# A planned kernel whose plan is replaced by a table: attention with a window and sinks, then a two-layer MLP, on one core

## The chip, the core and the metric

The kernel runs on one core of one Trainium2 chip. The metric is the device time of one execution in microseconds. Three runs of the kernel before gave 209.28 (the median), 208.73 and 210.27 us. The engines are named as in the profile: PE is TensorE (matmuls; PEld are its weight loads), DVE is VectorE, ACT is ScalarE, POOL is GpSimd and SP is SyncE. A name with a q behind it (SPq, POOLq, DVEq) is the instruction queue of that engine, which also issues DMAs.

## The reference

Four batches, eight heads, 768 positions, head width 64. Each position attends to the 128 positions of its window and to four sinks at the start of its sequence. The result, 4 x 768 rows of 512, is normalised and goes through a two-layer MLP with a residual.

```python
scores = scale * np.matmul(q, k.transpose(0, 1, 3, 2))          # q, k, v: (4, 8, 768, 64), scale 1/8
keep = (pos[None, :] < 4) | ((rel >= 0) & (rel < 128))          # rel = row - column
a = softmax(np.where(keep, scores, -1e9))
x = np.matmul(a, v)                                             # heads side by side: (4, 768, 512)
xn = (x - mean) / np.sqrt(var + 1e-06) * g_ln
out = x + np.maximum(xn @ w_ch1, 0.0) @ w_ch2                   # 512 -> 2048 -> 512
```

## The kernel before

**Tiling.** The 3072 rows are 24 tiles of 128 (t = 0 to 23), two to a chunk (c = 0 to 11), three chunks to a batch. A chunk goes through: load of q, k and v (POOL issues these DMAs, which also turn float32 into bfloat16); transposition of q and k to the tile `kq` (on PE with an eviction for chunks 0 to 3, L595, L672; by transposing DMAs on SP, L569, after that); scores on PE into a double PSUM bank (`pair`, L754 for the first four tiles, L802 later); exponent on ACT (`pe`, L758 and L814); mask on DVE (L761, L826; one in four on POOL in the second half); values on PE (L854) with the sinks (L721); then on DVE the reciprocal (L868), the scaling to `x` (L870), the statistics (L874, L876) and, with a power on POOL (L882, L883), the normalised tile `xc` (L885). `xc` is transposed to `xnt` (on PE with an eviction at L893 and L907 for chunks 0 and 1, by a transposing DMA after that). The MLP's first layer (on PE, L1020 and L1027) is followed by a ReLU on ACT or DVE (L1037, L1039). Its second layer is a plain product for chunks 0 and 1 (L1058). From chunk 2 on the second layer, and from chunk 4 on half of the first, is done with seven products of half-size blocks in place of eight, with the sums of blocks made on DVE (L1092 `hs`, L1123 `tm`, L1130 `ot`, L980 `hq`), POOL (L938 `xt`) and ACT (L969 `tz`, L983, L1001). SP stores the result (L1070, L1154, L1159).

**Buffers.** Every kind of tile has a ring of buffers: two double PSUM banks `pair`, four single ones `one`, ten `pe`, four `ot` and so on. What may start depends on the inputs and on the buffer being free.

**What sets the order.** Every piece of work is declared as an operation with its possible engines, an estimated duration, a priority and the buffers that it reads and writes (`P.op`). `Plan.run` then plays the whole kernel through on these estimates: it takes the operation that can start first, chooses its engine and its buffer, and goes on. The result is a start for each operation, and the instructions are emitted sorted by it. On the chip each engine works through its own list in that order, and waits by semaphores for what it needs. Names used below: `av` values product of a tile, `ev` eviction of a transposed q/k tile, `evx` the same of a normalised tile, `ex` exponent, `mk` mask, `vs` the sink values of a batch (L707 for batch 0, L539 for the rest), `vcd` the 16 small loads of sink values (L535), `w2t` and `wsum` and `w1g` preparations of the weights on DVE or ACT (L1178, L923, L1190), `p1` to `p7` the seven products of the second layer (L1109).

**Fillers.** Where the plan leaves PE idle in the first 24 us, matmuls on a tile of zeros (`junk`, L1236) are put in, as many as fit into the planned gap.

**The end.** The last chunk's four half tiles are stored by SP one by one (L1154), a one-column matmul (`late`, L1206) stands last on PE, and a count of bad reciprocals made earlier decides by a branch (L1240) whether a general version of the kernel has to run, which it does not here.

## Time and profile before

| | us |
|---|---|
| three runs: median, lowest, highest | 209.28, 208.73, 210.27 |
| profiled execution: span from the first to the last instruction | 206.6 |
| PE busy in it | 199.4 (97%) |
| DVE, ACT, POOL busy in it | 179.6, 119.7, 118.7 |
| granted TensorE clock | 1.000 |

The page gives the profiled execution by its span; the median of the runs is 2.7 us above that span. Busy shares are averages over the whole span. The kernel has a head of some 19 us, in which PE waits or works on fillers, a long body, and a tail from the last product to the last store.

### The profile page before, as it was taken

Reading aid. Unit: us, or ns where it says so; the run is one execution under the profiler, and the core shown is the slowest. Engines: PE = TensorE matmul, PEld = TensorE weight load, DVE = VectorE, ACT = ScalarE, POOL = GpSimd, SP = SyncE. Lnnn points to the kernel's source line nnn. Section 1 sums busy time; section 2 is a strip of 40 time slices with the busy share of each in tenths; the row PEclk is TensorE's granted clock in tenths of the full one; section 3 lists DMA queues with packets and bytes.
Section 4 is the critical chain, followed back from the end, with each engine's and each line's share of the span. In section 5 each row is a group of like instructions: output and inputs, shape, how many; then the busy total and the mean of one; then the engine's idle time right before and its main releaser. Section 6 shows DMA issues by size and latency. Waiting matters only on the chain.

```text
span 206.6 us, 6790 instructions
## 1 busy us (share of the span) xinstructions
PE 199.4 (97%) x2766; PEld 165.6 (80%) x2766; DVE 179.6 (87%) x437; ACT 119.7 (58%) x187; POOL 118.7 (57%) x170
## 2 busy tenths in 40 slices
PE   6888999999999999999999999999999999999994
PEld 2557996674698897898998988988988988988993
DVE  7589769899599899899989989989989989998693
ACT  3649477839555655666486486485486585560620
POOL 7977475279039029959649949968627229125000
PEclk9999999999999999999999999999999999999999
DMA  5999999999999999999999999899976411210302
GB/s 117 146 195 195 197 181 205 199 158 171 186 200 124 124 191 101 121 174 101 175 152 137 113 159 143 109 171 114 194 117 101 128 33 23 106 32 19 108 27 84
DMA packets 101341, 27.55 MB, mean 133 GB/s; under 512 B 89652, under 2 KB 99128, under 8 KB 101304
## 3 DMA queue, kind: packets, MB, share of 16 engines
q0 software_dynamic: 67712, 13.37, 81.7%
q1 hardware_dynamic: 33304, 13.43, 34.1%
q8 instruction: 22, 0.36, 0.7%
q10 hardware_dynamic: 288, 0.26, 0.4%
q14 instruction: 15, 0.12, 0.2%
HBM read 27.31 MB, written 6.29 MB: 163 GB/s over the span
## 4 chain that ended last, share of the span: by engine, by line
PE 90%; DMA 3%; DVE 3%; POOL 2%; issue 0%; DVEq 0%
PE one L1109 31%; PE one L1027 20%; PE one L958 12%; PE one L1058 7%; PE one L1020 7%; PE pair L854 5%; PE pair L802 4%; DMA n4b<-in_q_dram 3%; PE one L672 1%; PE pair L721 1%; POOL nat L626 1%; PE one L714 1%; DVE xnt L907 1%; DVE kq L595 1%; POOL vn L589 0%; DVE st L874 0%
## 5 line engine op out<-in xcount | busy, mean ns | idle before, releaser
L1027 PE MATMUL one<-xnt,w 128*128 128x256 bf16 x384 | 46.8, 273 | 0.0
L814 ACT ACTIVATE pe<-pair 128x1024 bf16<-128x1024 f32 (+1 forms) x40 | 36.3, 963 | 18.2 <-PE pair L802 18.2
L1037 ACT ACTIVATE hq<-one 128x512 bf16<-128x512 f32 x58 | 33.4, 590 | 17.9 <-PE one L1020 9.4
L1027 PEld LDWEIGHTS <-w 128*128 128x128 bf16 x384 | 36.3, 98 | 4.0
L1109 PEld LDWEIGHTS <-hs 128*128 128x128 bf16 x320 | 31.0, 98 | 4.0
L882 POOL TENSOR_SCALAR st<-st 128x1 f32<-128x1 f32 x24 | 6.4, 266 | 44.4 <-DVE rec L868 27.5
L826 DVE TENSOR_TENSOR pe<-pe,mask 128x1024 bf16<-128x1024 bf16 (+1 forms) x35 | 27.1, 799 | 1.6 <-ACT pe L814 1.4
L969 ACT COPY tz<-one 128x512 f32<-128x512 f32 x24 | 13.9, 585 | 20.6 <-PE one L958 19.2
L1109 PEld LDWEIGHTS <-hq 128*128 128x128 bf16 x240 | 22.2, 98 | 4.1 <-issue 0.5
L589 POOL DMA_DIRECT2D vn<-in_v_dram x24 | 21.9, 922 | 2.2 <-DMA w<-in_moe_w_ch_dram 1.2
L983 ACT ACTIVATE hq<-hq 128x512 bf16<-128x512 bf16 x24 | 15.1, 630 | 13.1 <-DVE hq L980 12.6
L1109 PE MATMUL one<-w,hq 128*128 128x256 bf16 x160 | 19.2, 273 | 0.0
L980 DVE TENSOR_TENSOR hq<-one,tz 128x512 bf16<-128x512 f32 x24 | 16.4, 684 | 1.9 <-PE one L958 1.0
L1130 DVE TENSOR_TENSOR ot<-one,tm 128x256 f32<-128x256 f32 x40 | 15.9, 412 | 2.1 <-PE one L1109 1.8
L1123 DVE TENSOR_TENSOR tm<-one,x 128x256 f32<-128x256 f32 x40 | 16.6, 414 | 1.2 <-PE one L1109 1.1
L870 DVE TENSOR_TENSOR x<-pair,rec 128x512 bf16<-128x512 f32 x24 | 16.6, 691 | 0.8
L874 DVE BATCH_NORM_STATS2 st<-x 128x6 f32<-128x512 bf16 x24 | 16.5, 687 | 0.2
L1020 PE MATMUL one<-xnt,w 128*128 128x128 bf16 x256 | 16.0, 219 | 0.5 <-DVE xnt L907 0.5
L687 POOL DMA_DIRECT2D nat<-in_q_dram x16 | 14.2, 893 | 3.7 <-DMA w<-in_moe_w_ch_dram 3.7
L938 POOL TENSOR_TENSOR xt<-xnt 128x256 bf16<-128x256 bf16 x16 | 12.2, 778 | 7.1 <-DMA xnt<-xc 7.0
L687 POOL DMA_DIRECT2D nat<-in_k_dram x16 | 14.8, 928 | 2.4 <-DMA w<-in_moe_w_ch_dram 2.4
L1020 PEld LDWEIGHTS <-w 128*128 128x128 bf16 x256 | 14.6, 98 | 1.6 <-issue 0.8
(130 smaller groups left out, 387.7 us busy)
## 6 DMA issues: line engine op xcount, KB each, us to landing
out_dram<-ot SPq DMA_DIRECT2D x17, 256.0 KB
w<-in_moe_w_ch_dram POOLq DMA_DIRECT2D x8, 512.0 KB, 12.8
vn<-in_v_dram POOLq DMA_DIRECT2D x24, 128.0 KB, 6.9
nat<-in_k_dram POOLq DMA_DIRECT2D x17, 128.0 KB, 4.6
nat<-in_q_dram POOLq DMA_DIRECT2D x17, 128.0 KB, 4.9
out_dram<-ot SPq DMA_DIRECT2D x14, 128.0 KB
kq<-nat SPq DMA_TRANSPOSE x32
xnt<-xc SPq DMA_TRANSPOSE x20
```

Source lines behind the costliest of these rows:

```text
L589: loads[b * RB + r, "v"] = P.op(f"vld{t}", {"POOL": (0.87, 0.9)}, prio, lambda e: G.dma_start(bv.t[:, :, 0:64], v[b, :, 128 * r:128 * (r + ...
L687: lambda e, nat=nat, ap=ap: G.dma_start(nat.t, ap), writes=[nat], dma=SW if c < 6 else (*SW[:2], PAR["llag"]), after=behind(c, 0 if soon e ...
L814: P.op(f"ex{c}{hp}", {"ACT": act(2 * n)}, d + 0.1 + 0.05 * j, lambda e, pp=pp, pb=pb: nc.scalar.activation(pb.t[:, :, 0:n], pp.t[:, :, 0:n ...
L826: V.tensor_mul(pb.t[:, :, 0:n], pb.t[:, :, 0:n], mm),
L870: P.op(f"x{t}", {"DVE": dve(512)}, d + xo + 0.11, lambda e: V.tensor_tensor(x.t.rearrange("p (a h c) -> p a h c", a=2, c=64), pv()[:, :, : ...
L874: P.op(f"bn{t}", {"DVE": fix(0.60)}, d + xo + 0.12, lambda e: V.bn_stats(st.t[:, 8:14], x.t), reads=[x], writes=[st, mv])
L958: nc.tensor.matmul(b.t[:, 128 * h:128 * h + 128], lhsT=lt[:, kk, 128 * h:128 * h + 128], rhs=rh[:, kk, :], start=first and h == 0 and kk = ...
L1020: nc.tensor.matmul(ph.t[:, 128 * s:128 * s + 128], lhsT=w1[u // 2][:, j, 128 * s:128 * s + 128], rhs=xnt.t[:, j, 128 * (u % 2):128 * (u % ...
L1027: nc.tensor.matmul(ph.t[:, 256 * s:256 * s + 256], lhsT=w1[ht // 4][:, j, 128 * (ht % 4):128 * (ht % 4 + 1)], rhs=xnt.t[:, j, :], start=j ...
L1037: nc.scalar.activation(hg.t[:, u % 4, :], ph.t, AF.Relu)
L1109: nc.tensor.matmul(at(r), lhsT=get(left, g)[:, v, s, :], rhs=rhs, start=first and n == 0, stop=n == 7, skip_group_check=True)
L1123: return P.op(f"tm{name}_{c}", {"DVE": dve(256, 1.14)}, pr - PAR["kp"], lambda e: V.tensor_tensor(tm[name].t, at(r), xs[i].t[:, sl], op=AL ...
```

## The change

`Plan.run` no longer plays anything through. A table, `SCHEDULE`, gives for each of the operations, in the order in which they are declared, an engine (P, A, V, G, S) and a start, and a second one, `SLOTS`, gives for each tile the buffer of its ring. The operations themselves, their instructions and their operands are the same. The lists of all five engines come out in another order, thirty operations change between ACT and DVE (the ReLUs, evictions and weight preparations that either can do), and nearly all buffers differ. The estimated durations of SP's operations are raised; since the start now comes from the table, they have a part only in the lives of the buffers by which fillers are placed.

```diff
     def run(self):
-        free = {"PE": 0.9, "ACT": 0.75, "DVE": 0.9, "POOL": 1.5, "SP": 0.75}
-        lanes = {"POOL": [0.0] * self.LANES, "HW": [0.0] * self.LANES}
...
-        while ready:
-            while tensor and tensor[0].start is not None:
-                tensor.pop(0)
...
-            e = min(cand, key=lambda e: min(c[0] for c in cand[e]))
-            t0 = min(c[0] for c in cand[e])
...
-        order.sort(key=lambda o: (o.start, o.seq))
-        return order
+        engines = dict(P="PE", A="ACT", V="DVE", G="POOL", S="SP")
+        table = SCHEDULE.split()
+        assert len(table) == len(self.ops)
+        for o, entry in zip(self.ops, table):
+            o.eng, o.start = engines[entry[0]], int(entry[1:]) / 100
+            o.end = o.start + o.engs[o.eng][1]
+        for b, n in zip(dict.fromkeys(b for o in self.ops for b in o.bufs if b.ring), "".join(SLOTS.split())):
+            b.slot = self.rings[b.ring][int(n, 36)]
+            for u in b.slot.units:
+                u.lives.append((min(o.start for o in b.users), max(o.end for o in b.users)))
+        return sorted(self.ops, key=lambda o: (o.start, o.seq))
...
+SCHEDULE = """
+V90 V103 V116 V162 G150 G180 V192 A181 V150 V144 V156 V324 V218 V212 V330 V963 V224 V235 V3027 V1987 V690 V835 V790
...
+SLOTS = """
+000100012300100000030111201113011223013041012323215060a852032065011351019410e94094101030120119106810a03030223704050129
...
-            P.op(f"vcd{g}{hh}", {"SP": (0.3, 0.3)}, 3.2 + 0.01 * (4 * g + hh), lambda e, p0=p0, h=4 * (g % 2) + hh: nc.sync.dma_start(
+            P.op(f"vcd{g}{hh}", {"SP": (0.36, 0.36)}, 3.2 + 0.01 * (4 * g + hh), lambda e, p0=p0, h=4 * (g % 2) + hh: nc.sync.dma_start(
...
-                    P.op(f"tr{nm}{c}{i}", {"SP": (1.2, 1.2)}, d + 0.01 * i, lambda e, nat=nat, i=i, x=x: dma_t(
+                    P.op(f"tr{nm}{c}{i}", {"SP": (1.32, 1.32)}, d + 0.01 * i, lambda e, nat=nat, i=i, x=x: dma_t(
...
-            P.op(f"st{t}{half}", {"SP": (0.35, 0.4)}, 3000.0 + half % 2 if c == NC - 1 else u(6), lambda e, i=half // 2, b=b, r=r, sl=sl: nc.sync.dma_start(
+            P.op(f"st{t}{half}", {"SP": (0.45, 0.45)}, 3000.0 + half % 2 if c == NC - 1 else u(6), lambda e, i=half // 2, b=b, r=r, sl=sl: nc.sync.dma_start(
```

The change was announced with two more phrases, that SyncE's last stores stand in order of need and that ScalarE's function table is fetched first. On ACT the program begins in both versions with two DMAs and then the table load. The last four stores follow their producers in both.

Three places of the new order are shown. Line numbers of the changed kernel are lower by 19 here, as the planner's code is gone.

**DVE in the head.** This is DVE before, from the evictions of the second tile's q and k (L595, banks `one_65` and `one_66`) to the first normalised tile and the two evictions that follow.

```order
L595 COPY kq_85<-one_65 128x4x128
L595 COPY kq_85<-one_66 128x4x128
L531 COPY gt<-one_63 128x4
L868 RECIPROCAL rec<-pair_61 128x8
L870 TENSOR_TENSOR x_104<-pair_61,rec 128x512
L874 BN_STATS st_158<-x_104 128x6
L876 BN_AGGR st_158<-st_158 128x2
L885 TENSOR_SCALAR xc_116<-x_104,st_158 128x512
L595 COPY kq_86<-one_64 128x1024
L907 TENSOR_TENSOR xnt_122<-one_66,gt 128x4x128
```

And this is DVE after, from the same reciprocal to the same normalised tile's eviction; the eviction of bank `one_65` stands three rows ahead of the first row shown, with two rows that build `pick` between. `x_104`, `st_158` and `xc_116` are the first tile's x, statistics and normalised tile, and `x_105`, `st_159` and `xc_117` the second's.

```order
L849 RECIPROCAL rec<-pair_61 128x8
L469 MEMSET kts_102 128x96
L851 TENSOR_TENSOR x_104<-pair_61,rec 128x512
L576 COPY kq_85<-one_66 128x4x128
L855 BN_STATS st_158<-x_104 128x6
L857 BN_AGGR st_158<-st_158 128x2
L866 TENSOR_SCALAR xc_116<-x_104,st_158 128x512
L676 COPY kts_102<-kq_85 64x4x4 x2
L512 COPY gt<-one_63 128x4
L888 TENSOR_TENSOR xnt_122<-one_66,gt 128x4x128
```

The second eviction of the second tile (`one_66`) now stands behind the first tile's `x`, and the 1024-wide eviction of chunk 1 (`kq_86`) has gone to ACT. Further on, up to the eviction of the second normalised tile, a mask (L761) has moved from behind `xc_117` to ahead of its statistics' end, and the sink values `vs_182` (L707) have moved from behind that eviction to ahead of it.

**SP's first loads and transposes.** SP before, from its first row of work:

```order
L526 DMA g_187<-in_moe_g_ln_dram 4x128
L535 DMA vc<-in_v_dram 4x3x64 x16
L1070 DMA out_dram<-ot_154 128x512
L569 DMA_TRANSPOSE xnt_124<-xc_120 128x4x128
L569 DMA_TRANSPOSE xnt_124<-xc_121 128x4x128
```

SP after:

```order
L507 DMA g_187<-in_moe_g_ln_dram 4x128
L550 DMA_TRANSPOSE xnt_122<-xc_120 128x4x128
L550 DMA_TRANSPOSE xnt_122<-xc_117 128x4x128
L516 DMA vc<-in_v_dram 4x3x64
L550 DMA_TRANSPOSE kq_88<-nat_70 128x4x128
L550 DMA_TRANSPOSE kq_88<-nat_72 128x4x128
L550 DMA_TRANSPOSE kq_88<-nat_77 128x4x128
L550 DMA_TRANSPOSE kq_88<-nat_74 128x4x128
L516 DMA vc<-in_v_dram 4x3x64 x12
```

The 16 loads of sink values have left the head of SP's list. They now stand behind and between the transposes of chunks 2 and 4, the first of which waits for the normalised tiles of chunk 2.

**DVE in the last chunk.** DVE before, from the first block sum (`hs`) of the last chunk to its first finished half tile (`ot`):

```order
L1092 TENSOR_TENSOR hs_136<-hq_132 128x512
L1092 TENSOR_TENSOR hs_139<-hq_132 128x512
L1092 TENSOR_TENSOR hs_137<-hq_131 128x512
L1092 TENSOR_TENSOR hs_142<-hq_131 128x512
L1092 TENSOR_TENSOR hs_134<-hs_137,hq_131 128x512
L1123 TENSOR_TENSOR tm_153<-one_64,x_115 128x256
L1092 TENSOR_TENSOR hs_135<-hs_139,hq_132 128x512
L1130 TENSOR_TENSOR ot_156<-one_63,tm_153 128x256
```

DVE after, from the same place:

```order
L1073 TENSOR_TENSOR hs_140<-hq_127 128x512
L1073 TENSOR_TENSOR hs_139<-hq_127 128x512
L1073 TENSOR_TENSOR hs_141<-hs_139,hq_127 128x512
L1073 TENSOR_TENSOR hs_137<-hq_131 128x512
L1073 TENSOR_TENSOR hs_136<-hq_131 128x512
L1104 TENSOR_TENSOR tm_152<-one_66,x_110 128x256
L1073 TENSOR_TENSOR hs_143<-hs_136,hq_131 128x512
L1073 TENSOR_TENSOR hs_138<-hq_127,hs_141 128x512
```

On PE the products of the last chunk stood in the order p1, p2, p7, p6, p4, p5, p3 and now stand as p1, p7, p6, p4, p5, p3, p2. So the half tile that p2 finishes comes first before and last after. The sum that p6 needs is the row `hs_135` before and `hs_143` after. In both it stands behind the first `tm`, which waits for p1; before, p2 and p7 stood between p1 and p6 on PE, and now p7 alone does.

More of the change, by code (lines that the diff above doesn't have):

```diff
@@ L207, in pe @@
+PE_DRAIN = 0.18
 def pe(us):
-    return {"PE": (us, us + Plan.PE_DRAIN)}
+    return {"PE": (us, us + PE_DRAIN)}
 def act(n):
@@ L232 @@
 HW_T = (0.10, 0.8, 0.8)
-Plan.DMA_BUSY = {SW: 1.03, HW_X: 0.55}
 LOW, HIGH = 1e-9, 1e9
```

168 lines of the change are left out of this document (72 added, 96 removed).

## The prediction

> **What bounds the kernel now.** I read the page's totals first, then PE's busy time by stretch, then the chain that ended last, and at last PE's waits.
>
> ```profile
> span 206.6 us, 6790 instructions
> PE 199.4 (97%) x2766; PEld 165.6 (80%) x2766; DVE 179.6 (87%) x437; ACT 119.7 (58%) x187; POOL 118.7 (57%) x170
> 0.00:18.75 18.75, 14.57 (x194) 9.14 (x195) 13.83 (x50) 10.21 (x14) 14.95 (x25) 1.00 1.29 160
> 18.75:203.45 184.70, 184.63 (x2570) 156.40 (x2569) 165.30 (x388) 109.46 (x174) 103.72 (x145) 1.00 1.18 131
> ```
>
> The last two rows give a stretch, its length, then the busy time of PE, PEld, DVE, ACT and POOL. PE is busy for 184.63 of 184.70 us after 18.75: 0.07 us are idle there. In front of 18.75 it is busy for 14.57, fillers among them. The change leaves PE's products alone, so the body cannot become shorter. It can only get waits, and a gain can come from the first 18.75 us or from what follows the last product. The chain shows what each of these two ends hangs on.
>
> ```profile
> 5.50 7.09 DMA n4b<-in_q_dram
> 12.60 0.14 issue
> ...
> 13.41 1.23 DVE kq L595
> ...
> 18.01 0.70 DVE xnt L907
> 18.71 0.04 issue
> 18.75 1.05 PE one L1020 x16
> ...
> 69.71 1.75 PE one L1027 x16
> ...
> 197.29 6.13 PE one L1109 x56
> 203.45 0.44 DVE ot L1130
> ```
>
> The head is a load (`n4b`, landed at 12.60), a transposition on PE, its 1.23 us eviction on DVE, and behind that on the same engine the two normalised tiles' evictions (`xnt`; the second at 18.01) with one tile's softmax end and normalisation between them. The second starts the packed body at 18.75. The tail is the last product, its sum on DVE at 203.45, and a store to the end, 206.6 - 203.45 = 3.15 us. The span is therefore head 18.75, body 184.70, tail 3.15. The median of the runs, 209.28, is 2.68 above the span; I work with differences and add them to that median.
>
> **The head: +0.15 us.** These are the rows for DVE and PE there.
>
> ```profile
> 8.25 0.76 DVE L595 COPY kq<-one 128x512 bf16<-128x512 bf16 x2 [0.21 <-PE one L645]
> 10.96 0.69 DVE L870 TENSOR_TENSOR x<-pair,rec 128x512 bf16<-128x512 f32 x1
> 14.55 0.68 DVE L907 TENSOR_TENSOR xnt<-one,gt 128x512 bf16<-128x512 bf16 x1
> 17.32 0.69 DVE L761 TENSOR_TENSOR pe<-pe,mask 128x1024 bf16<-128x1024 bf16 x1
> 18.01 0.69 DVE L907 TENSOR_TENSOR xnt<-one,gt 128x512 bf16<-128x512 bf16 x1
> 19.21 0.42 DVE L707 TENSOR_TENSOR vs<-one,sel 128x260 bf16<-128x260 f32 x1
> 10.45 0.92 PE L1236 MATMUL one<-junk 128*128 128x512 bf16 x5
> 11.73 0.40 PE L754 MATMUL pair<-kq 64*128 64x128 bf16 x8
> 12.73 1.08 PE L672 MATMUL one<-ident,n4b 128*64 128x128 bf16 x32 [0.60 <-DMA n4b<-in_q_dram]
> 13.75 0.40 PE L893 MATMUL one<-ident,xc 128*128 128x128 bf16 x4
> ```
>
> The second tile's `one_66` eviction is one of the pair at 8.25, so 0.76 / 2 = 0.38 us. Now it stands behind the first `x`, which ends at 10.96 + 0.69 = 11.65, and ends at 12.03. The scores at 11.73 read it, so they cannot end at 11.73 + 0.40 = 12.13 but about 12.03 + 0.40 = 12.43. More fillers stand around these scores, three of 128 columns ahead and one of 512 with three of 128 behind. By the five at 10.45 one of 512 columns takes 0.92 / 5 = 0.18, so I put the lot behind the scores at 0.32 to 0.38 as an estimate. The transposition of `n4b` then starts at 12.75 to 12.9 where it started at 12.73: the wait of 0.60 for the load hides nearly all. I take 12.9, and L893 at 13.9 for 13.75. L893 ends at 14.3, and with the 1.23 us eviction gone to ACT the first `xnt` can start there, 0.25 before its 14.55.
>
> From the first `xnt` to the second is 18.01 - 14.55 = 3.46 us, already with the mask of 17.32 inside. The sink values (`vs`, 0.42 at 19.21) come in front of the second; on DVE the next row starts some 0.08 before the last one's listed end (14.55 against 13.41 + 1.23 = 14.64), so 0.34. The second `xnt` starts at 14.3 + 3.46 + 0.34 = 18.10 for 18.01. With 0.70 and 0.04 behind it PE would start the body at 18.84. Two more fillers of 512 columns stand in front of that group on PE, up to 0.36 if they come late; I count 0.06 of it. The head is +0.15. Bounds: -0.25, the gain of the first `xnt` alone if `vs` were hidden, and +0.6, which is 0.09 with the fillers' 0.36 and 0.15 for a second step of the same size as L893's delay.
>
> SP's 16 small loads leave the head.
>
> ```profile
> 3.96 0.90 POOL L589 DMA_DIRECT2D vn<-in_v_dram  x1
> 3.64 7.97 SPq L535 DMA_DIRECT2D vc<-in_v_dram  x16
> q0 software_dynamic: 3900, 0.79, 141.2%
> q1 hardware_dynamic: 163, 0.05, 4.0%
> 48.09 4.97 SPq L1070 DMA_DIRECT2D out_dram<-ot  x2
> 60.34 3.65 SPq L569 DMA_TRANSPOSE xnt<-xc  x2
> ```
>
> Rows three and four are the DMA queues in the stretch 3.6 to 10.2: packets, megabytes, time of the packets over 16 engines' time. The whole second queue is 4.0% of 6.6 us, 0.26 us, and that bounds what the head's loads can gain. In the new order 12 of these loads stand in one piece on SP behind chunk 4's `kq` transposes and ahead of the two `xnt` transposes of 60.34; at 7.97 / 16 = 0.50 each that is 6.0 us. The two stores of 48.09, 4.97 us, leave the same place, so the transposes come about 1 us later. They ended at 63.99 and chunk 3's first layer reads them at 69.71: 5.7 us of cover, and I count nothing. If the whole 6.0 came on top, PE would wait 0.3.
>
> **The middle: +0.4 us.** Between the reading of chunk 2's `x` and the first half-size `tm` DVE gets more to do.
>
> ```profile
> 40.80:63.70 22.90, 22.90 (x235) 15.92 (x231) 19.97 (x48) 12.62 (x19) 12.86 (x19) 1.00 1.97 175
> 63.70:79.70 16.00, 16.00 (x241) 13.32 (x239) 14.64 (x36) 9.84 (x15) 7.47 (x11) 1.00 1.48 134
> L826 DVE TENSOR_TENSOR pe<-pe,mask x35: 548/683/1328, 33.6 to 175.7; 128x1024 bf16<-128x1024 bf16 x23, 128x768 bf16<-128x768 bf16 x12
> L1178 DVE TENSOR_TENSOR w2t<-w,n4c 128x512 bf16<-128x512 bf16 x4 | 1.7, 420 | 0.1
> L1190 DVE TENSOR_SCALAR w<-w,gt 128x512 bf16<-128x512 bf16 x8 | 3.0, 417 | 1.0 <-PE one L1020 1.0
> L1039 DVE TENSOR_SCALAR hq<-one 128x512 bf16<-128x512 f32 x6 | 4.1, 689 | 0.2
> L1092 DVE TENSOR_TENSOR hs<-hq 128x512 bf16<-128x512 bf16 x40 | 15.0, 418 | 0.8 <-ACT hq L1037 0.6
> ```
>
> DVE's busy time, the third figure, leaves 22.90 - 19.97 = 2.93 and 16.00 - 14.64 = 1.36 us, together 4.29. Into this stretch the new order puts three more weight scalings (L1190, 0.417), five more weight sums (L1178, 0.420), two more ReLUs (L1039, 0.689) and one more mask (L826, 0.683, the middle figure), and takes one `hs` (0.418) out: 1.25 + 2.10 + 1.38 + 0.68 - 0.42 = 4.99 us. These are counted by listed lengths; with neighbours overlapping by up to 0.08, ten rows net are 4.2 to 5.0. DVE has no slack left there, and PE waits for what it lacks: 0 to 0.7, of which I take the middle, 0.35, and 0.05 for a row that comes in the wrong place. The lower bound is 0: 18.75 to 203.45 has only 0.07 to win. The upper bound is the slower rival's 2.6.
>
> **The tail: +0.15 us.** PE's order of the last seven products changes.
>
> ```profile
> 202.37 1.04 PE L1109 MATMUL one<-w,hs 128*128 128x256 bf16 x8
> 202.57 0.42 DVE L1123 TENSOR_TENSOR tm<-one,x 128x256 f32<-128x256 f32 x1 [0.45 <-PE one L1109]
> 202.91 0.96 DVE L1130 TENSOR_TENSOR ot<-one,tm 128x256 f32<-128x256 f32 x2
> ```
>
> One product is 6.13 / 7 = 0.876 (56 matmuls in the chain). p6 needs a sum which stands on DVE behind the first `tm`, and that waits for p1. Counted from p1's start: p1 ends at 0.876; `tm` starts 0.20 into the following product (202.57 against 202.37), at 1.08; the row behind it starts 0.34 later (202.91), at 1.42; the sum takes 0.418 and PE follows 0.05 later, at 1.89. PE is ready after p1 and p7, at 1.75. That is +0.14, so +0.15. Before, p2 stood between as well, and 1.89 was covered by 2.63. Bounds: 0, if `tm` follows at once (202.57 came 0.20 late for a reason of its own), and +0.4, if a sum of the same length comes ahead. The last product's `ot` and store are the same rows, so 3.15 us stay. The table load of ACT stands in the same place of its list, behind two DMAs, and costs nothing either way.
>
> **Sum:** 0.15 + 0.4 + 0.15 = +0.7. The span becomes 207.3, the time 209.28 + 0.7 = 210.0. Likeliest case's own range: 209.3 to 211.0.
>
> **Rivals.** *Slower: DVE full, and its masks long.* The 35 masks spread from 548 to 1328 ns. By their share some 35 x 38.9 / 142.1 = 9.6 of them lie in the middle stretch. Where DVE has no slack, a long mask is no longer hidden: four at 1.328 for 0.683 are +2.6, one is +0.65. This rival decides from two such masks more than before (+1.3). For it speaks the zero slack; against it that half of the masks ran in 683 or less. Time: 209.28 + 0.3 + 0.65 to 2.6, so 210.9 to 212.2, middle 211.6. The Trainium skill ("SBUF — State Buffer", "Who interferes with whom") says that VectorE and GpSimd share a pair of ports as an exclusive lock and that the loser waits for the whole instruction. The mask's spread agrees with it, though no run here shows which POOL row held it.
>
> *Faster: the head's loads land earlier.* PE's long wait is for the first values, `vn` issued at 3.96, and for `n4b` at 12.60. With the 16 small loads away both may come up to 0.26 earlier; with the `vs` hidden, the head is -0.26, and with no wait in the middle or the tail the time is 209.0. Against it: the first `xnt` now hangs on `one_66` and the fillers as well. The Trainium skill ("DMA: Bandwidth & Descriptors", "Queues, rings and completion order") says that each DMA engine takes queues in turn, a packet at a time. By that rule the small queue would hold the large one by its share of turns and not of bytes; 163 packets against 3900 make that no more than the row's 4%.
>
> *Nothing: the table gives the same waits.* All terms 0, 209.3; it takes that DVE's overlaps cover all ten rows.
>
> **How the numbers follow.** Forecast (+0.7) 0.55; DVE rival 0.22; loads rival 0.13; nothing 0.06; something unseen, such as a wait on a buffer of the new table, 0.04, above 212.4. About 1% (2.1 us) is what a measurement of this kernel can tell from no change. A gain over 1% would need 2.1 us out of the head, whose bound is 0.26: 0.05 for an error of my reading. Slower by over 1%, above 211.4: over half of the DVE rival, the unseen case and a little of the forecast, 0.22. Within: 0.73. The range, 208.6 to 212.4, takes the loads rival's 209.0 with the 0.4 by which runs differ downwards, and the DVE rival's end.
>
> **What would show it.** Right: the packed body starts at 18.8 to 19.0 in the changed trace; DVE's idle time in the middle is below 0.5 and PE lists waits for DVE of 0.2 to 0.7 in sum; in the tail a wait of 0.1 to 0.2 of the third product for `hs`, and 3.15 from the last product. Wrong: a body start at or below 18.5; PE waiting in the middle for a DMA or for ACT; masks of 1.3 us in the middle more than two oftener than before; or a body without waits.

## The result and the profile after

The changed kernel takes 214.85 us (median of four runs, 213.38 to 215.61) against 209.35 us for the kernel before beside it: **slower, 1.0272 times, 95% interval 1.0214 to 1.0329**, some 5.5 us. The forecast was 210.0 with a range up to 212.4. The profiled execution is the fastest of the four, 213.38 us; its span is 211.8, so it is 5.2 us longer than the one before. Line numbers in the changed kernel are lower by 19. One slow run of a later experiment (the small loads late in the kernel before, 219.26 us) is left out of its median and its ratio.

These are the page's totals after.

```profile
span 211.8 us, 6770 instructions
PE 200.7 (95%) x2767; PEld 165.3 (78%) x2773; DVE 179.2 (85%) x441; ACT 117.2 (55%) x186; POOL 117.3 (55%) x170
```

And, as in the prediction, stretches with their length and the busy time of PE, PEld, DVE, ACT and POOL: up to the start of the packed body, to the last `ot`, and to the end.

```profile
0.00:18.30 18.30, 15.34 (x200) 9.50 (x202) 11.92 (x47) 11.14 (x15) 14.72 (x25) 1.00 1.28 159
18.30:206.65 188.35, 185.25 (x2568) 155.78 (x2572) 166.82 (x394) 106.06 (x172) 102.61 (x145) 1.00 1.16 129
206.65:211.80 5.15, 0.08 (x2) 0.00 (x0) 0.42 (x1) 0.00 (x0) 0.00 (x0) 0.77 0.23 76
```

Before, the three stretches were 18.75, 184.70 and 3.15 us. So the head is 0.45 shorter, the body 3.65 longer with 3.10 us in which PE does nothing (0.07 before), and the tail 2.0 longer. PE's busy time in the body is 0.62 higher too, with no more matmuls. The ends of matmuls are modelled in the profile, and a product that a wait splits is listed longer: the one that waits at 22.81 has 0.19 and 0.61 us around its wait, and 0.65 in one piece before. PE's waits name what ended the idle time in the body (us in total, times, longest):

```profile
PE one L1090 <- DVE tm L1104: 1.1, 3, 0.4
...
PE one L1008 <- DVE ot L1111: 0.6, 1, 0.6
PE pair L835 <- DMA vn<-in_v_dram: 0.5, 1, 0.5
PE one L1090 <- DVE ot L1111: 0.3, 1, 0.3
PE one L1090 <- DVE hs L1073: 0.2, 1, 0.2
```

Before, no row of this kind had its place behind 18.75, except the last one-column matmul's. The chain of waits shows the first two of three places in order of time (start, us, what):

```profile
10.16 12.61 DMA vn<-in_v_dram
22.81 0.61 PE pair L835 x15
...
29.23 1.01 PE one L653 x32
...
55.61 5.56 DMA kq<-nat
61.19 0.42 DMA vc<-in_v_dram
61.72 0.88 POOL nat L668
...
62.98 0.58 POOL st L864
63.59 0.41 DVE xc L866
...
66.31 1.02 SPq L516
67.37 0.38 SPq L1051
67.81 2.41 DMA out_dram<-ot
70.79 1.03 PE one L1008 x8
```

First, PE starts the body 0.45 earlier and loses that again at 22.81, where the fourth tile's values product waits for `vn`. The transposition of chunk 2, behind the same groups of the first layer in both orders, starts at 29.23; before it was this row of the chain:

```profile
29.12 1.01 PE one L672 x32
```

So head and early body together are +0.11 in these two traces. The figure is uncertain: in the eleven traces of the changed kernel and its variants below, the transposition of chunk 2 starts between 28.84 and 30.59 (29.59 in the mean), in the four of the kernel before and its variants between 28.67 and 29.32 (29.02). The head may thus cost half a us more than this pair shows; that is not settled. Second, between 55 and 71 us the chain runs through SP: transposes and the small loads of sink values (L516), then a POOL load that waits for a buffer, the power on POOL behind it and DVE's `xc`; and again small loads, a store that waits behind them, and an `ot` on DVE that waits for the store to have read its buffer. Third, from the last `ot` to the end there are now 5.15 us.

For a comparison without the head's scatter I use the stretch from the first matmul of chunk 2's transposition to the last `ot`, by the trace's records: 174.40 us before, 177.49 after. In four traces whose order is that of the change up to `late` it is 177.32 to 177.81, so differences under 0.5 us in one trace say little. The account of the 5.2 us is then 0.11 + 3.09 + 2.01.

### The profile page after: what moved, and what is told of

Its sections match the earlier page's. It is cut to its first block, busy times and chain, and to the rows that moved or that the text cites. A ratio compares the mean times of both kernels' runs of the same rounds, so it can differ in the third digit from the quotient of the medians.

```text
span 211.8 us, 6770 instructions
## 1 busy us (share of the span) xinstructions
PE 200.7 (95%) x2767; PEld 165.3 (78%) x2773; DVE 179.2 (85%) x441; ACT 117.2 (55%) x186; POOL 117.3 (55%) x170
## 4 chain that ended last, share of the span: by engine, by line
PE 69%; DMA 10%; DVE 7%; POOL 5%; SPq 3%; ACT 2%; issue 2%; DVEq 0%; POOLq 0%
PE one L1090 23%; PE one L1008 15%; PE one L939 11%; DMA vn<-in_v_dram 6%; PE one L1001 5%; PE one L1039 5%; PE pair L835 4%; DVE hs L1073 3%; DMA kq<-nat 3%; PE pair L783 2%; SPq L550 2%; DVE pe L807 1%; DMA out_dram<-ot 1%; DVE tm L1104 1%; POOL w L528 1%
## 5 line engine op out<-in xcount | busy, mean ns | idle before, releaser
L1018 ACT ACTIVATE hq<-one 128x512 bf16<-128x512 f32 x53 | 31.0, 595 | 21.9 <-PE one L1008 14.4
L795 ACT ACTIVATE pe<-pair 128x1024 bf16<-128x1024 f32 (+1 forms) x40 | 36.8, 961 | 10.5 <-PE pair L783 10.5
L1008 PEld LDWEIGHTS <-w 128*128 128x128 bf16 x384 | 36.4, 98 | 4.7 <-issue 1.0
L1090 PEld LDWEIGHTS <-hs 128*128 128x128 bf16 x320 | 30.2, 98 | 6.4 <-issue 1.3
L807 DVE TENSOR_TENSOR pe<-pe,mask 128x1024 bf16<-128x1024 bf16 (+1 forms) x35 | 24.6, 717 | 1.8 <-ACT pe L795 1.8
L1090 PEld LDWEIGHTS <-hq 128*128 128x128 bf16 x240 | 22.9, 98 | 4.0 <-issue 0.8
L1090 PE MATMUL one<-w,hq 128*128 128x256 bf16 x160 | 20.3, 273 | 0.0
L1073 DVE TENSOR_TENSOR hs<-hq 128x512 bf16<-128x512 bf16 x40 | 15.8, 419 | 3.2 <-ACT hq L1018 1.5
L668 POOL DMA_DIRECT2D nat<-in_q_dram x16 | 14.8, 927 | 4.4 <-DMA w<-in_moe_w_ch_dram 3.4
L939 PEld LDWEIGHTS <-hq 128*128 128x128 bf16 x256 | 15.8, 98 | 0.3
```

The costliest lines, as they stand in the source:

```text
L668: lambda e, nat=nat, ap=ap: G.dma_start(nat.t, ap), writes=[nat], dma=SW if c < 6 else (*SW[:2], PAR["llag"]), after=behind(c, 0 if soon e ...
L795: P.op(f"ex{c}{hp}", {"ACT": act(2 * n)}, d + 0.1 + 0.05 * j, lambda e, pp=pp, pb=pb: nc.scalar.activation(pb.t[:, :, 0:n], pp.t[:, :, 0:n ...
L807: V.tensor_mul(pb.t[:, :, 0:n], pb.t[:, :, 0:n], mm),
L939: nc.tensor.matmul(b.t[:, 128 * h:128 * h + 128], lhsT=lt[:, kk, 128 * h:128 * h + 128], rhs=rh[:, kk, :], start=first and h == 0 and kk = ...
L1008: nc.tensor.matmul(ph.t[:, 256 * s:256 * s + 256], lhsT=w1[ht // 4][:, j, 128 * (ht % 4):128 * (ht % 4 + 1)], rhs=xnt.t[:, j, :], start=j ...
L1018: nc.scalar.activation(hg.t[:, u % 4, :], ph.t, AF.Relu)
```

## Experiments: the tail

**The last one-column matmul behind the last half tile.** In the kernel before, `late` (L1206) waits for the half tile of p3, the last product there. The change makes p2 the last product, and `late` still waits for p3's half.

```diff
-        last_sum[:] = [ots[0], oo[1]]
+        last_sum[:] = [ots[0], oo[0]]
...
-        late.t[0:1, 0:1], lhsT=last_sum[0].t[:, 511:512], rhs=ones_f, start=True, stop=True),
+        late.t[0:1, 0:1], lhsT=last_sum[0].t[:, 255:256], rhs=ones_f, start=True, stop=True),
```

(and the entry of `late` in the table from 201.48 to 202.05, behind that `ot`).

> The changed kernel with one edit: the last one-column matmul on PE (late) waits for the half tile that p2 finishes, which is now the last one, where it waited for the half that p3 finishes. Nothing else moves. Theory A (PE's instruction fetch): in the changed kernel late runs at 206.54, 0.1 us before the last ot row begins; PE goes through its branch and fetches 16 KB of instructions at 208.19, 1.12 us after the last ot ends, while the last store is still on the DMA engines, and the share of one engine lands at 210.83 where the others are done by 208.8. With late behind the last ot the fetch starts about 0.5 us later, all shares land about 1.7 us after the last ot, and from the start of the last ot to the end of the span there are 3.2 us where there were 5.15: the time falls by 1.8 to 2.2 us, to about 212.8. Rival B (the last store is late for its own reason, such as the load on the DMA engines or a slow receipt): the tail stays at 4.7 to 5.2 us and the time within 0.5 of the changed kernel's.

Measured: 1.0147 (1.0081 to 1.0212) times the kernel before, 211.8 us. Here is `late` in PE's timeline, of the changed kernel and then of this one, where the bracket shows its wait:

```profile
206.54 0.19 PE L1187 MATMUL one<-ones_f,ot 128*1 128x1 f32 x2
```

```profile
206.84 0.19 PE L1187 MATMUL one<-ones_f,ot 128*1 128x1 f32 x2 [0.52 <-DVE ot L1111]
```

This is the stretch from its last `ot` to the end:

```profile
206.37:209.50 3.13, 0.19 (x2) 0.09 (x2) 0.42 (x1) 0.00 (x0) 0.00 (x0) 0.99 0.37 124
```

The tail is 3.13 us again. The DMA queues show what happened in between (packets, megabytes, share of the 16 engines). Of the changed kernel, the first two rows are the stretch 208.1 to 208.3 and the last is 209.0 to 210.8:

```profile
q1 hardware_dynamic: 69, 0.06, 92.8%
q8 instruction: 1, 0.02, 46.2%
...
q1 hardware_dynamic: 9, 0.01, 2.7%
```

And of the kernel with the edit, 208.2 to 209.8:

```profile
q8 instruction: 1, 0.02, 3.8%
q14 instruction: 2, 0.02, 3.2%
```

An instruction fetch of 16 KB (the queue q8) starts in the middle of the last store, at 208.19. Nine packets of the store's 144, one sixteenth and so by their number one engine's share, move only after 209.0. By the packets' own records the fetch ends at 209.66 and the first of the nine starts at 209.65. The same stands in all five traces with a tail of 4.88 us or more: 135 packets of the last store go ahead, and the last nine start within 0.02 us of the fetch's end. With the edit the fetch starts at 208.59 by the DMA records, and no packet of the store's queue is left.

**The opposite edit in the kernel before,** and **the same delay by work in place of a wait.**

```diff
-        last_sum[:] = [ots[0], oo[1]]
+        last_sum[:] = [ots[1], oo[3]]
```

> The kernel before with the opposite edit: late waits for the half tile that p5 finishes, so it does not wait for the last ot. Theory A: late runs at about 203.35 where it ran at 203.93, the fetch starts about 1.1 us after the last ot's end where it was 2.0, meets the last store on one DMA engine, and the tail grows from 3.15 to between 4.5 and 5.2 us: time 209.3 + 1.3 to 2.0, that is 210.6 to 211.3. Rival B: the tail stays at 3.15 and the time at 209.3; late's place is without effect.

Measured: 1.0003 (0.9972 to 1.0035); tail 3.43. The forecast of theory A for this kernel was wrong: `late` ran early, at 203.07, but the tail grew by 0.3 only.

```diff
-    P.op("late", pe(0.06), 4000.0, lambda e: nc.tensor.matmul(
-        late.t[0:1, 0:1], lhsT=last_sum[0].t[:, 511:512], rhs=ones_f, start=True, stop=True),
+    P.op("late", pe(0.06), 4000.0, lambda e: [nc.tensor.matmul(
+        late.t[0:1, 0:1], lhsT=last_sum[0].t[:, 511:512], rhs=ones_f, start=True, stop=True)] + [nc.tensor.matmul(
+        late.t[:, 0:512], lhsT=junk[:, 0:128], rhs=junk[:, 0:512], start=True, stop=True) for _ in range(1)],
```

> The changed kernel with late where the change has it, and one more matmul of 512 columns on zeros behind it on PE (0.2 to 0.4 us), so that PE comes to its branch that much later without waiting for any half tile. Theory A (only the time at which PE's instruction fetch starts against the last store counts): the fetch starts 1.3 to 1.5 us after the last ot's end where it was 1.12. That is the gap at which the kernel before with the early late lost 0.3 us, so the tail from the last ot's start is between 3.1 and 3.6 us where it was 5.15. Rival B (late's wait for the half tile itself is what helps): the tail stays at 4.7 to 5.2.

> As the one before with three such matmuls (0.65 to 1.2 us). Theory A: the fetch starts 1.7 us or more after the last ot's end, behind the store; tail 3.1 to 3.2 us (end of the span possibly 0.1 later by PE itself). Rival B: tail 4.7 to 5.2.

Measured: one run each, 213.98 and 213.25 us, tails 4.90 and 5.05. Taken literally that is rival B, but neither run made the test: the fetch did not move (1.11 and 1.12 us after the last `ot`). In the second, PE's branch stands at 207.10 by the records, ahead of the last of the three matmuls, which starts at 207.17. The wait holds PE's instruction stream; this much work does not. All the tails together, by the records:

| kernel | last ot ends | fetch starts | between | tail |
|---|---|---|---|---|
| before | 203.87 | 205.85 | 1.98 | 3.14 |
| changed | 207.07 | 208.19 | 1.12 | 5.15 |
| changed, late behind p2 | 206.79 | 208.59 | 1.80 | 3.11 |
| before, late early | 203.56 | 205.05 | 1.49 | 3.43 |
| changed, one matmul more | 207.93 | 209.04 | 1.11 | 4.90 |
| changed, three more | 207.14 | 208.26 | 1.12 | 5.05 |
| changed, small loads ahead (below) | 206.10 | 207.21 | 1.11 | 4.88 |
| changed, fills on POOL (below) | 205.81 | 207.10 | 1.29 | 5.22 |

A fetch up to 1.29 us behind the last `ot` costs 1.7 to 2.1 us, one from 1.49 on 0.3 or nothing. In the kernel before with the early `late`, the fetch starts at 205.05, the moment at which the last packet of the store ends; there the store came first, so the collision was not made in the kernel before. In eleven of the fifteen traces the fetch starts 1.14 to 1.17 us behind PE's branch, in this one 1.39 and in three more 1.32 to 1.74; why is open.

## Experiments: SP's list

**The 16 small loads back ahead of the transposes.** Only their entries in the table change, to 30.00 to 35.40, when SP has nothing else to do.

```diff
-vcd00 S4886  vcd01 S5485 ... vcd30 S5961  vcd31 S6272  vcd32 S6308  vcd33 S6344
+vcd00 S3000  vcd01 S3036 ... vcd30 S3432  vcd31 S3468  vcd32 S3504  vcd33 S3540
```

> The changed kernel with the 16 small loads of sink values back ahead of SP's transposes (planned at 30 us; SP has nothing else to do there), all else in the table unchanged. Theory A (SP's list): in the changed kernel the 12 loads hold SP from 56.9 to 62.8 and three more from 65.5 to 67.3; the transposes and stores behind them come late, and with them the POOL loads that wait for nat buffers, the power on POOL behind these (xc of the eighth tile at 63.59, 1.2 us after DVE was ready for it) and the ot buffers (DVE waits 0.9 us for the store's landing until 70.3). PE loses 0.47 us at 66.40 and 0.69 at 70.79. With the loads gone both waits go and the time falls by 0.9 to 1.3 us. Rival B (DVE is simply full there): the waits stay, at another row, and the time falls by less than 0.3. If later waits absorb part of it (DVE's lag is caught up by a stall further on), the gain is between.

Measured: 1.0175 (1.0113 to 1.0236), 0.0097 less than the change, or 2.0 us by the medians' ratio; in the trace the stretch from chunk 2's transposition to the last `ot` is 176.06, 1.43 us less. The wait for `ot` at 70.79 is gone; at 66.5 some 0.15 us is left. The rest of the 2.0 is within the scatter of the runs. Part of the 1.43 is the wait at 175.87, which this trace lacks; it comes and goes (see the section on POOL's masks).

**The small loads late in the kernel before.** One of them behind chunk 2's transposes, twelve ahead of the `xnt` transposes of chunk 3, three behind; its stores keep their places. Its planner's starts are overwritten ahead of the sort:

```diff
+        late = [49.0] + [55.2 + 0.25 * i for i in range(12)] + [61.4, 61.5, 61.6]
+        for o in order:
+            if o.name.startswith("vcd"):
+                o.start = late.pop(0)
+            elif o.name == "vs1":
+                o.start = 65.5
         order.sort(key=lambda o: (o.start, o.seq))
```

> The kernel before with the 16 small loads on SP at the places that the change gave them: one behind the transposes of chunk 2, twelve in one piece ahead of the xnt transposes of chunk 3, three behind these; the sink values of the second batch (vs) go later on DVE so that they follow. The stores keep their places. Theory A (SP's list makes POOL and DVE late): the transposes at 60.34 start about 6 us later, POOL's loads of the next chunk and DVE's xc behind, and PE loses 0.5 to 1.3 us between 62 and 80 where it lost nothing: time 209.0 + 0.5 to 1.3. Rival B (the kernel before has slack enough in this stretch, since its stores went out earlier): PE's waits there are below 0.2, the time within 0.3.

Measured: 1.0307 (1.0257 to 1.0356), 215.40 us: five times the upper price. The chain around PE's wait, and the page's granted clock in 40 slices of the span, in tenths:

```profile
65.68 8.35 DMA xnt<-xc
74.03 0.05 issue
74.08 3.59 PE one L1033 x16
...
PEclk9999999999999759999999999999999999999999
```

PE waits for 4.63 us, and that is not the whole price: the 16 matmuls behind the wait take 3.59 us, where the same ones took 1.75 before (the row at 69.71 in the prediction). By the trace's records the granted clock is 0.50 from 72.52 to 79.35. The stretch from chunk 2's transposition to the last `ot` is 182.08 us, 7.68 more than before.

SP's queue from 60 us on:

```profile
60.04 4.26 SPq L541 DMA_DIRECT2D vc<-in_v_dram  x12
64.39 4.27 SPq L575 DMA_TRANSPOSE xnt<-xc  x2
```

And the DMA queues, two rows of the stretch 70.0 to 71.5 and two of 72.0 to 74.0:

```profile
q0 software_dynamic: 1785, 0.22, 265.8%
q1 hardware_dynamic: 6, 0.00, 0.6%
...
q1 hardware_dynamic: 1309, 0.32, 133.7%
q0 software_dynamic: 87, 0.01, 8.2%
```

The transposes begin 4.05 us later than at 60.34, and the second lands only at 74.03, 8.35 us after its issue at 65.68 by the chain. In the 1.5 us from 70.0 POOL's loads move 1785 packets and SP's queue 6; the transposes move when the loads are done. The Trainium skill ("DMA: Bandwidth & Descriptors", "Queues, rings and completion order") says that a DMA engine with work in several queues takes them in turn, packet by packet; these rows do not look like turns. Whether the transposes' packets were already queued then, the trace does not show.

So the place of the small loads on SP is not free in either kernel. In the changed one the stores had been moved behind the transposes too, which kept the transposes' own start (62.91 against 60.34) near its place; there the price was paid by POOL's buffers and by the stores.

## Experiments: POOL's masks beside DVE's sums

These rows are DVE, POOL and PE of the changed kernel around 113 us.

```profile
112.24 0.41 DVE L1073 TENSOR_TENSOR hs<-hs,hq 128x512 bf16<-128x512 bf16 x1
112.57 0.86 DVE L1073 TENSOR_TENSOR hs<-hq,hs 128x512 bf16<-128x512 bf16 x1
113.35 1.12 DVE L807 TENSOR_TENSOR pe<-pe,mask 128x1024 bf16<-128x1024 bf16 x1
114.39 0.41 DVE L1104 TENSOR_TENSOR tm<-one,x 128x256 f32<-128x256 f32 x1
...
112.39 1.53 POOL L802 TENSOR_SCALAR_AFFINE_SELECT pe<-pe 128x512 bf16<-128x512 bf16 x2 [0.20 <-ACT pe L795]
...
114.86 1.03 PE L1090 MATMUL one<-w2t,hq 128*128 128x256 bf16 x8 [0.39 <-DVE tm L1104]
```

A sum of 0.41 takes 0.86 and a mask of 0.68 takes 1.12 while POOL masks another tile, and the `tm` behind them, for which PE waits, comes 0.9 us late. The same stands at 128.63 (two sums in 1.64 us) and at 173.85 (one in 0.85).

**Fills in place of POOL's masks,** in the changed kernel and in the kernel before.

```diff
-                            G.affine_select(out=v, in_=v, compare_op=(ALU.is_gt, ALU.is_ge)[u], fill=0.0, base=0,
-                                            pattern=[[0, 4], [2 * u - 1, 128]], channel_multiplier=1 - 2 * u)
+                            G.memset(v, 1.0)
```

> The changed kernel with the five masks that stand on POOL replaced by fills with ones of the same places (twice half the tile, as the mask's two passes). This leaves out the mask of one pair of heads in chunks 5, 7, 8, 10 and 11, so the softmax of these is without meaning; everything else is computed. The point: POOL's mask reads and writes SBUF, a fill only writes. Theory A (DVE and POOL keep each other out): the sums hs of 0.42 us which took 0.85 to 0.86 at 112.57, 128.63, 129.41 and 173.85 beside POOL's masks, and the masks of 1.12 beside them, fall back to 0.42 and 0.68; PE's waits at 114.86 (0.46), 129.5 to 131.0 (0.7 in sum) and 175.87 (0.4) go, and the time falls by 1.0 to 1.6 us. Theory B (DVE's list is simply too full there, the long rows hit where there is slack): the rows may get shorter, but PE's waits fall by less than a third and the time by less than 0.5. If only the fill's shorter length matters, the rows beside the fills stay at 0.6 to 0.85.

> The kernel before with the same fills in place of POOL's five masks (the same part of the softmax is left out). In it POOL's masks ran at 80.65, 110.41, 125.94, 155.73 and 171.07 beside DVE's masks, which took 1.09 to 1.33 us there, and PE waited for nothing. Theory A (the collisions are as many before, but fall on rows with nothing urgent behind them): DVE's masks there fall to 0.68, the time stays within 0.3 of the kernel before, body 184.4 to 184.8. Rival B (they cost before too, spread over many places): the time falls by 0.6 or more.

Measured: the changed kernel 1.0129 (1.0065 to 1.0193), 0.0143 less than without the fills; the stretch from chunk 2's transposition to the last `ot` 175.84, 1.65 us less. The same place:

```profile
112.87 0.41 DVE L1072 TENSOR_TENSOR hs<-hq,hs 128x512 bf16<-128x512 bf16 x1
113.20 0.68 DVE L806 TENSOR_TENSOR pe<-pe,mask 128x1024 bf16<-128x1024 bf16 x1
...
112.68 0.99 POOL L802 MEMSET pe<- 128x512 bf16 x2 [0.18 <-ACT pe L795]
```

PE's waits at 114 and at 129 to 131 are gone. So is the one at 175, but it is also missing in the trace with only `late` moved, whose masks are on POOL, so that one does not tell. By the ratio the gain is 3.0 us and in the stretch 1.65; the head's scatter is in the first. A fill is also shorter than a mask (0.99 us for 1.53), and how much of the gain comes from that alone was not tried. The kernel before with the fills: 0.9995 (0.9964 to 1.0025), no change, although its DVE mask at 110.56 had been stretched to 1.09 and now takes 0.69:

```profile
110.56 1.09 DVE L826 TENSOR_TENSOR pe<-pe,mask 128x1024 bf16<-128x1024 bf16 x1
111.58 0.41 DVE L1123 TENSOR_TENSOR tm<-one,x 128x256 f32<-128x256 f32 x1
```

```profile
111.13 0.69 DVE L825 TENSOR_TENSOR pe<-pe,mask 128x1024 bf16<-128x1024 bf16 x1
```

Both kernels have such collisions. Rows that stand beside POOL and are over 0.15 us longer than the median of their line and shape add up to 6.6 us before (20 rows) and 7.8 after (21 rows). In the rows shown, the sums of the kernel before stand ahead of POOL's mask, which starts at 110.41, and the `tm` behind it had time; in the changed kernel a sum and a mask stand beside POOL's mask, ahead of the `tm` that PE waits for. This is read from the order and was not tried apart.

The Trainium skill ("SBUF — State Buffer", "Who interferes with whom") says that a VectorE instruction with two inputs in SBUF contends with a GpSimd instruction that reads SBUF, not with one that only writes it. The runs agree: 0.86 beside the mask, 0.41 beside the fill.

**Other places on DVE, and the masks on DVE.** Both on top of the two repairs above (`late` behind p2, small loads ahead). First three rows change places:

```diff
-mk71 V10965  mk81 V12392  tmt1_9 V17008
+mk71 V11090  mk81 V12500  tmt1_9 V16960
```

> As the one before, and on DVE three rows change places in the table: the masks mk71 and mk81 go behind the sums that the next products wait for, and the tm row of chunk 9's first product ahead of one sum. POOL's masks stay where they are and still collide with DVE's rows. Theory A (the collision costs PE only through what is queued behind the long rows): PE's waits at 114.2 (0.56), 129.2 to 130.7 (0.28, 0.34, 0.22) and, where it shows, 175 shrink to under 0.4 in sum, the long rows of 0.85 stay in the trace at another row, the body is 185.8 to 186.2 us and the ratio about 1.000. Rival B (DVE is full: what one row gains the next loses): the waits move to the values products, which wait for the masks, and the body stays above 186.6.

Then also POOL's five masks go to DVE:

```diff
-mkp=(0,)
+mkp=()
...
-mk50 G  mk70 G  mk80 G  mk100 G  mk110 G
+mk50 V7920  mk70 V11150  mk80 V12700  mk100 V15670  mk110 V17193
```

> The changed kernel with late behind p2's half tile, the 16 small loads ahead of SP's transposes, the three DVE rows of the earlier run in their new places, and POOL's five masks made by DVE as a multiplication like its other masks, each behind a tm row; nothing is left out. Theory A (it is the collision with POOL's masks that costs, about 0.43 us for each of DVE's sums that meets one, and it falls ahead of what PE needs): PE's waits at 114, 129 to 131 and 175 are below 0.3 in sum, the rows of 0.85 beside POOL's masks are gone, body 185.2 to 186.2, ratio 0.999 to 1.005. Rival B (DVE has no room there, whoever holds it): five more rows of 0.68 on DVE cost what the collisions cost, the waits move to the values products and the sums behind the masks, body 186.6 to 188.0 and ratio 1.008 to 1.016.

Measured: 1.0104 (1.0069 to 1.0139) with the rows moved, against 1.0112 (1.0066 to 1.0157) without (the next section): nothing gained; PE waits 0.7 at 130.4 in one piece, and waits stand at 109.4 and 176 (one at 109.8 is also in the trace with only `late` moved). Masks on DVE: 1.0067 (1.0041 to 1.0094), between the two forecasts; its body in the trace, 187.4 us, is in rival B's range, but this trace is the slowest of its eleven runs. The waits at 114 and at 129 to 131 are gone, but six of 0.1 to 0.3 us have come at other places. By the ratios it is a gain of 0.4%, and the intervals overlap. So it is shown that POOL's masks cost the changed kernel PE time; that DVE has no room to take them at no price rests on one trace. How much of the 1.65 us is the collision and how much the lack of room is not separated.

## Experiments: the sum

The two edits together, `late` behind p2 and the small loads ahead, with the diffs shown above:

> The changed kernel with both edits that were tried alone: late waits for p2's half tile, and the 16 small loads stand ahead of SP's transposes. Theory A (two costs of separate places): they add. The tail from the start of the last ot is 3.1 us (5.15 in the changed kernel), the stretch from the second group of the first layer (the start of the packed body) to the last ot 186.9 us (188.35 in the changed kernel, 184.7 before), and the ratio to the kernel before about 1.005 (1.027 for the changed kernel, less 0.0125 for the one and 0.0097 for the other). Rival B (one waits for what the other hid): the ratio stays at 1.012 or more.

In addition the three DVE rows and, on PE, the fourth tile's values product behind one more group of the first layer:

```diff
-ph0_5 P2221  av3 P2173
+ph0_5 P2172  av3 P2240
```

> As the one before, and the values product of the fourth tile stands behind one more group of the first layer on PE, as before the change (there it ran at 23.84; in the changed kernel it stood at 22.3 and waited for vn until 22.81). Theory A: the wait of 0.2 to 0.5 us for vn goes, body 185.3 to 185.8. Rival B: the groups of the first layer need weights that land at about 25.7 at the earliest, so PE, being 0.4 us earlier, waits for these in its place and the body gains less than 0.15. Ratio 0.997 to 1.002.

And the two edits with the fills on POOL:

> The changed kernel with all three costs that were tried apart taken away: late behind p2's half tile, the 16 small loads ahead of SP's transposes, and POOL's five masks replaced by fills with ones (so that pair of heads is unmasked in chunks 5, 7, 8, 10 and 11; all else is computed). Theory A (tail, SP's list and the collisions of POOL with DVE are the whole loss): body 185.0 to 185.7 us, tail 3.1, ratio to the kernel before 0.998 to 1.004. Rival B (a further cause in the table's order, such as DVE too full or the weights landing late): the body stays above 186.2 and the ratio above 1.006.

Measured, in this order: 1.0112 (1.0066 to 1.0157), 1.0107 (1.0071 to 1.0143) and **0.9967 (0.9938 to 0.9996)**. The first missed its forecast of 1.005, though tail (3.12) and body (186.93) came out as theory A has them: its packed body starts at 19.38, 1.1 us later than in the changed kernel's trace. The second stayed far above its 0.997 to 1.002. The third is theory A's, with the body a little below its range (184.9).

| kernel | to chunk 2's transposition | from there to the last ot | tail |
|---|---|---|---|
| before | 29.05 | 174.40 | 3.14 |
| changed | 29.16 | 177.49 | 5.15 |
| changed, late behind p2 | 29.05 | 177.32 | 3.11 |
| changed, small loads ahead | 29.61 | 176.06 | 4.88 |
| changed, fills | 29.55 | 175.84 | 5.22 |
| both edits | 30.30 | 176.01 | 3.12 |
| both, rows moved | 29.28 | 176.88 | 3.12 |
| both, rows and values product moved | 30.07 | 176.42 | 3.12 |
| both, masks on DVE | 30.59 | 176.17 | 3.12 |
| both edits and fills | 28.84 | 174.69 | 3.12 |

With all three taken away the stretches are those of the kernel before, to 0.3 us. The three costs of the trace add up: 177.49 less 1.43 and 1.65 is 174.41, against 174.69 measured. By the ratios the three edits singly give 2.6, 2.0 and 3.0 us and together 6.4; these figures hold the head's scatter as well. This is the last kernel of the table, in the stretches of the first section:

```profile
0.00:18.64 18.64, 15.68 (x200) 9.56 (x202) 12.37 (x47) 11.14 (x15) 14.94 (x26) 1.00 1.29 161
18.64:203.53 184.89, 184.29 (x2566) 155.69 (x2570) 163.39 (x394) 106.08 (x172) 98.84 (x145) 1.00 1.20 131
203.53:206.65 3.12, 0.19 (x2) 0.09 (x2) 0.43 (x1) 0.00 (x0) 0.00 (x0) 1.00 0.37 125
```

With the values product in its old place the wait for `vn` is absent (0.5 in the changed kernel), but so it is in the trace of both edits without that move, whose head is as late (body from 19.38 and from 19.50); 0.2 us of waiting for the weights stood at 26.1. There is no gain, and the run does not decide between its theories.

The last kernel leaves the work of POOL's masks out; of those that compute everything, none is faster than the kernel before.

## Why the prediction was wrong, step by step

- **What bounds the kernel: right.** The body could only get waits, and got 3.1 us of them.
- **Head, +0.15: near in size by luck, wrong in its steps.** Chunk 2's transposition came 0.11 later in the profiled pair. The body started at 18.30, which the prediction itself names as a sign of being wrong. The sum began with the first `x` at 10.96; it ran at 10.38, behind a values product at 9.60 for 10.19, and the scores behind the moved eviction at 11.46 for 12.03. The fillers behind them took 0.48 us, more than the 0.32 to 0.38 put down. The product that had moved ahead then met `vn`'s landing; I had compared PE's order only up to the start of the body. In other traces the changed order starts its body at up to 19.50 us.
- **Faster rival, loads earlier: not shown.** The first values landed at 8.92 us for 10.15 and `n4b` at 12.06 for 12.60, more than its 0.26. But in another trace of the old head, with the 16 loads in it (`late` early), they landed at 8.70 and 12.02, so this is scatter between runs.
- **SP's small loads, "I count nothing": wrong, 1.4 us in the trace.** My cover was counted to the end of the transposes' issue and not to their landing, and for one reader. I left out who else waits behind SP: POOL's loads for the buffers that the transposes read, the power behind these loads, and DVE for the stores' buffers. The prediction's fallback, 0.3 us if the whole 6.0 came on top, was far too small: in the kernel before 4.05 us of delay cost a wait of 4.6 and a halved clock behind it.
- **The middle, +0.4: wrong in its count and place; 0.1 to 0.2 us was left at 66 once SP's part was taken away.** Ten rows more were there (three scalings, five weight sums, two ReLUs), but five rows (`hs`, `tm`, `ot`) had slipped behind 79.70. DVE's busy time rose from 34.61 to 34.86 us and not by 4.2 to 5.0, and its idle time was 4.04, not under 0.5; DVE waited itself. I stopped the count at 79.70.
- **The slower rival: right in its mechanism and wrong in its stretch.** DVE rows stretched beside POOL did become PE's waits, but behind 80 us, and on the sums more than on the masks. In the trace they cost 1.65 us; the rival's price was 0.65 to 2.6 (its lower time, 210.9, goes with two long masks, 1.3; with 0.65 its own sum gives 210.2). Its chance, 0.22, was too small: I had looked at one stretch, and the order of DVE against POOL's masks is new behind it as well.
- **The tail, "3.15 us stay": wrong, 2.0 us.** I checked that the same rows stand behind the last product. I did not ask what `late` waits for. It was the wait that kept PE's instruction fetch behind the last store, and the new order of the products took it away. The +0.15 for p6's sum did not show: there is no wait of 0.1 or more of PE there.
- **The range.** Its upper end held the one rival; two more mechanisms, of 1.4 and 2.0 us, had been given no price.

## What to carry to other kernels

Where an order changes, each instruction that waits is to be asked what else its wait holds back: a matmul that seems idle at the end may be there to keep its engine's branch behind the last store. A DMA queue's list is to be followed to every buffer that its transfers free, and the cover counted to the landing. And where one engine lengthens another's rows, the number of collisions said little here; by the order, what stands behind the row that is hit decides.

## What the runs showed of the hardware

**PE's rate in the first microseconds.** One filler of 512 columns follows another after 0.43 us at first and after 0.22 later. In fifteen traces the change comes with the first record of the granted clock, between 4.48 and 7.67 us. In front of it there is no record, and the profile's rows read 1.00 all the same. Here is PE at the first transposition (L630) in the changed kernel, and then in the one with both edits, whose head is the same:

```profile
5.17 0.76 PE L1217 MATMUL one<-junk 128*128 128x512 bf16 x5
5.85 0.62 PE L630 MATMUL one<-ident,hq 128*128 128x128 bf16 x8
```

```profile
5.66 1.38 PE L1217 MATMUL one<-junk 128*128 128x512 bf16 x5
6.83 0.70 PE L630 MATMUL one<-ident,hq 128*128 128x128 bf16 x8
```

Five fillers of 0.76 us take 1.38, and the first transposition is 0.98 later. In the kernel before this had no effect, since the transposition of `n4b` waits for its load (12.16 to 12.95 in four traces of it, with first transpositions from 5.75 to 6.93). In the changed one it follows the first transposition directly, at 12.27 to 13.47, and the body starts between 18.30 and 19.50 in eleven traces. Whether it also widens the scatter of its runs is not shown. The Trainium skill ("TensorE: Matmul & The Clock Gate", "Part 1: The HAM clock gate (the "warmup" mystery)") says that the array's clock is halved until a free-running window of about 3.4 us has been busy, so that the moment differs from run to run. The traces agree in the halved rate and in the scatter. They do not agree in the length: the first filler is at 1.85, and in six of them the change comes only 2.6 to 3.2 us behind it.

**An engine's instruction fetch shares the DMA engines with the stores.** A 16 KB fetch took 0.9 to 1.5 us, and the nine packets of a store that stood behind it made the tail some 2 us longer. **In a long wait of PE the granted clock fell to a half.** In the kernel before with the small loads late it was 0.50 from 72.52, 3.1 us into the wait of 4.63 us, until 79.35, 5.3 us behind it. **An engine's sequencer runs ahead of matmuls that wait for nothing:** up to three 512-column matmuls ahead of PE's branch did not delay it.
